# A gated mix of a state-space layer and an FFN on one core: slot 3 and the odd FFN tiles as pairs, another order at the start, the last read-out in two halves

## The chip, the core and the metric

The kernel runs on one core of a Trainium2 chip. Five engines work side by side, each through its own instructions in order, with semaphores between them: TensorE (PE; its weight loads are shown as PEld), VectorE (DVE), ScalarE (ACT), GpSimd (POOL) and SyncE (SP, which here only issues DMAs). Matmul results go to PSUM, which has eight banks of 128 x 512 float32 here; VectorE or ScalarE copies them out ("evicts" them) before a bank can be written again. The metric is the time of one execution on the device, in microseconds. The median of three runs of the kernel before is 145.91 us (145.41 to 146.05).

## What is computed

`x` has 2048 tokens of 448 features. Two branches are mixed by a gate per token: a diagonal complex state-space layer (a recurrence over the tokens with 448 states) and a feed-forward network with 1792 hidden features.

```python
x = A_x
g = _sigmoid((x * gate_w).sum(-1, keepdims=True))
# branch a
dt = exp(log_dt); Lam = Lambda_re + 1j * Lambda_im
Lam_bar = exp(dt * Lam)
B_bar = ((Lam_bar - 1.0) / Lam)[:, None] * (B_re + 1j * B_im)
Bu = einsum("bld,pd->blp", x, B_bar)
for t in range(L):
    h = Lam_bar[None, :] * h + Bu[:, t, :]
a = 2.0 * einsum("blp,dp->bld", hseq, Cmat).real + x * Dskip
# branch b
b = silu(x @ w1) @ w2
return g * a + (1 - g) * b
```

## The kernel before

**Tiling.** Tokens come in four chunks of 512 (`CH`), sixteen blocks of 128. The 448 states, real and imaginary, are seven slots of 128 partitions: slots 0, 1, 2 real and 4, 5, 6 imaginary parts of 384 states, slot 3 the last 64 states' real parts in its lower and imaginary parts in its upper 64 partitions. Slot 7 of `U` and `Gb` is slot 3 with its halves swapped. The FFN has fourteen tiles of 128 hidden features.

**The state-space branch.** For each chunk PE makes the seven slots of `B x` (BU), which are evicted to `U`. `lanes` (L659) then works on VectorE: products of `U` with cosines and sines of the states' phases turn the complex recurrence into a real one, seven `tensor_tensor_scan` instructions (L670) run it, ScalarE copies each scan result to `Gb` (L673), products turn it back into `H` (two buffers, by the chunk's parity). For each block of tokens, `readout` (L720) multiplies `H` with the read-out weights `CP` (L731), VectorE sums the result with the other branch (`tf`, L725; `ot`, L734), and SP stores it (L737). Each scan starts from the end of the chunk before.

**The FFN branch.** F1 makes the fourteen hidden tiles, ScalarE evicts them with Silu into `aT` (L695); F2 (`ffn2`, L700) multiplies them with `w2` for each block of tokens (fourteen matmuls, L706), ScalarE scales by 1 - g into `Tb` (L710).

**Pairs.** The contraction over 448 features is three and a half blocks of 128. `step` (L601) therefore makes two output tiles at a time with matmuls of 64 rows, two of which lie side by side in the array (L595). A pair's first half has eight matmuls, its second six: fourteen, against sixteen of half a block. The second half is emitted behind the first half of the next pair; `close` ends an open pair. A pair holds two PSUM banks from its first half until both tiles are evicted. Per chunk there are three BU pairs (0,1), (4,5), (6,2) and seven F1 pairs (k, 7 + k). Slot 3 is left over: `bu_last` (L639) makes it alone, with four matmuls over 128 rows (L644).

**The order of the work.** PE runs in the order in which the program adds its steps, written out by hand at the end (L796 to L862). The other engines' orders come from a planner (`Plan.order`, L102): with estimated costs it starts on each engine what can begin first, and of several that can begin at once the one with the lowest number `prio`. `Waits` then adds the semaphore waits. What an engine does is thus fixed in order, and an instruction that waits holds back all behind it.

**The start.** SP issues in order: the first 512 rows of x (one DMA, L372), B in four DMAs (L373 to L376), w1 in ten, w2 in one, then two transposing DMAs for chunk 1 of `xT` (L386), then C. ScalarE's queue issues the four parameter rows `prm` (L358). PE first runs 15 matmuls on zeros (`idle`, L415). Then it transposes x (L435; evicted at L439 to L443), then the parameters (L459, L461), for which VectorE first repeats 64 columns of `prm` (L453); then B: slots 0 and 1 (B01), two idle matmuls, slots 4 to 6 (B456). Then come BU(0,0), slots 2 and 3 (B23), the other BU pairs, F1(0,0), slot 3 and the gates of chunk 0. B's transposes are evicted at L576 (ScalarE) and L578 (VectorE) into `BT`. From the parameters, VectorE and ScalarE make phases `ph` and decays `rc` (L471 to L475); then ScalarE loads the table that has Silu and Sin (L476).

**The phases.** For each of four groups of states a ramp of 512 times the phase is made in `Gf`: b = 0 and 1 by ScalarE (L493), b = 2 and 3 by GpSimd (L496). VectorE takes the nearest whole number (L479) and subtracts it (L482); ScalarE takes the sine (L504, L507, L509), VectorE the absolute value (L511), ScalarE from that the cosine (L512). VectorE copies them for slots 4 to 6 (L514, L515).

**Lines at the seams.** `late_loads` (L392) issues the remaining x once chunk 0's swapped `Gb` is there. `swapped` (L634) copies slot 3 to slot 7 with two DMAs. `readout_weights` (L740) makes `CP` from C behind chunk 1's F1. The last seven lines of PE's order are F2(12), C(8), and so on to C(11), then C(12) to C(15) in a row: the last of these, its sum on VectorE and its store end the run.

Of the kernel before, what the change touches and what calls it, by code (L numbers as in the profile page):

```python
# [261 lines left out]
def bass_gated_mix__ssm_conv_s5__dense_activation_silu__prompt_kernel(nc, A_x, A_Lambda_re, A_Lambda_im, A_B_re, A_B_im, A_C_re, A_C_im,  # L262
               A_log_dt, A_Dskip, B_x, B_w1, B_w2, gate_w, out):
    with ExitStack() as ctx:
# [3 lines left out]
        def sb(name, shape, dtype):  # L268
            return E(nc.sbuf_tensor(name, list(shape), dtype))
# [34 lines left out]
        prm = sb("prm", [4, 512], BF16)  # L304
# [122 lines left out]
        def x_transposes(n):  # L427
            tk = Ps()

            def mm(pe):  # L430
                for q in range(2):
                    i = 2 * n + q
                    for b in range(4):
                        o = (q * 4 + b) * 128
                        r = pe.transpose(bk16(tk)[:, o:o + 128], xnat[:, b, XCOL[i]:XCOL[i] + 128], ident[:, :])  # L435
                return r
            P.add("pe", mm, ["xn0", "ident"], [tk], 0.5)
            if n == 0:
                DVE(lambda e: e.tensor_copy(xT[:, 0:2, 0:CH], bk16(tk)[:, :].rearrange("p (q n) -> p q n", q=2)),  # L439
                    [tk], ["xT00"], 0.7, 2)  # L440
            else:
                ACT(lambda e: e.activation(xT[:, 2, 0:CH], bk16(tk)[:, 0:CH], AF.Copy), [tk], ["xT01"], act_cost(512), 1)
                DVE(lambda e: e.tensor_copy(xT[:, 3, 0:CH], bk16(tk)[:, CH:2 * CH]), [tk, "xT01"], ["xT02"], 0.42, 2)  # L443

        x_transposes(0)
        x_transposes(1)

        def xr(tc):
            return [f"xT{tc}{k}" for k in range(2 if tc else 3)]


        prmn = [f"prm{k}" for k in range(4)]
        DVE(lambda e: e.tensor_copy(prm[:, 448:512], prm[:, 384:448]), prmn, ["prmd"], 0.2, 1)  # L453
        tk = Ps()

        def prm_t(pe, tk=tk):
            for b in range(4):
                lanes = prm[0:4, b:384:3] if b < 3 else prm[0:4, 384:512]
                pe.transpose(bk16(tk)[:, 4 * b:4 * b + 4], lanes, ident[0:4, 0:4])  # L459
            for b in range(3):  # L460
                r = pe.transpose(bk16(tk)[:, 16 + 4 * b:16 + 4 * b + 4], prm[0:4, 128 * b:128 * b + 128], ident[0:4, 0:4])  # L461
            return r
        P.add("pe", prm_t, prmn + ["prmd", "ident"], [tk], 0.3)
# [25 lines left out]
        for b in range(4):  # L489
            q = b % 2  # L490
            dst = Gf[:, b, :]
            if b < 2:
                ACT(lambda e, b=b, dst=dst: e.activation(dst, itf[:, :], AF.Copy, scale=ph[:, b:b + 1]),  # L493
                    ["itf", "ph"], [f"Gf{b}"], act_cost(512, 1), 2)
            else:
                POOL(lambda e, b=b, dst=dst: e.tensor_single_scalar(dst, itf[:, :], ph[:, b:b + 1], ALU.mult),  # L496
                     ["itf", "ph"], [f"Gf{b}"], 1.65)
            DVE(nearest(wk[q], dst), [f"Gf{b}"], [f"Gf{4 + q}"], dve_cost(512, 2), 3)
            DVE(minus(dst, dst, wk[q]), [f"Gf{b}", f"Gf{4 + q}"], [f"Gf{b}"], dve_cost(512), 3)
# [59 lines left out]
        def b_transposes(slots, reads, h, to_act):  # L559

            tk = Ps()
            n = len(slots)

            def mm(pe):
                for q in range(2):
                    i = 2 * h + q
                    for j, s in enumerate(slots):
                        o = (q * n + j) * 128
                        r = pe.transpose(bk16(tk)[:, o:o + 128], Bnat[:, s, XCOL[i]:XCOL[i] + 128], ident[:, :])  # L569
                return r  # L570
            P.add("pe", mm, reads + ["ident"], [tk], 0.06 * 2 * n)
            dst = BT[:, 2 * h:2 * h + 2, slots[0] * 128:(slots[-1] + 1) * 128]
            src = lambda: bk16(tk)[:, 0:2 * n * 128].rearrange("p (q m) -> p q m", q=2)
            name = f"BT{h}_{slots[0]}"
            if to_act:
                ACT(lambda e: e.activation(dst, src(), AF.Copy), [tk], [name], act_cost(256 * n), 0)  # L576
            else:
                DVE(lambda e: e.tensor_copy(dst, src()), [tk], [name], 0.1 + 0.00058 * 256 * n, 0)  # L578

        B01, B23, B456 = (0, 1), (2, 3), (4, 5, 6)  # L580
        b_transposes(B01, ["Bn0"], 0, False)
        b_transposes(B01, ["Bn0"], 1, True)
        idle(2)
        b_transposes(B456, ["Bn3"], 0, False)
        b_transposes(B456, ["Bn3"], 1, True)
        b01, b23, b456 = ([f"BT{h}_{s}" for h in range(2)] for s in (0, 2, 4))
# [4 lines left out]

        def half_steps(pe, w, xc, a, b, lo, hi, start):
            for i in range(len(lo)):
                for p0, (tk, c0), k in ((0, a, lo[i]), (64, b, hi[i])):
# [6 lines left out]
        def step(pair):  # L601

            w, tc, ca, cb, reads, evict = pair
            a, b = Ps("pair"), Ps("pair")
            xc = tc * CH
            begin = lambda pe: half_steps(pe, w, xc, (a, ca), (b, cb), (0, 1, 2, 3), (0, 1, 2, 3), True)
            end = lambda pe: half_steps(pe, w, xc, (b, cb), (a, ca), (0, 1, 2), (0, 1, 3), False)
            reads = reads + xr(tc)
            P.add("pe", begin, reads, [a, b], 0.87, rows=64)
# [28 lines left out]

        def bu_last(tc):  # L639
            tk = Ps()  # L640

            def mm(pe):
                for i in range(4):
                    r = pe.matmul(bk(tk), BT[:, i, 384:512], xT[:, i, tc * CH:(tc + 1) * CH],  # L644
                                  start=(i == 0), stop=(i == 3))
                return r
            P.add("pe", mm, b23 + ["BT3z"] + xr(tc), [tk], 0.87)
            u_out(3, tk)
            if tc:
                swapped(U, "U", 0)  # L650
            else:
                for k, p in ((0, 0), (1, 64)):
                    DVE(lambda e, p=p: e.tensor_copy(U[p:p + 64, 7, :], U[64 - p:128 - p, 3, :]),  # L653
                        ["U3"], [f"U7{'ab'[k]}"], dve_cost(512, 4), 2)
# [37 lines left out]
        def ffn1_pair(tc, k):  # L692
            def evict(a, b):
                for tk, fb in ((a, k), (b, 7 + k)):
                    ACT(lambda e, tk=tk, fb=fb: e.activation(aT[tc % 2][:, fb, :], bk(tk), AF.Silu),  # L695
                        [tk, "tbl"], [f"aT{tc % 2}_{fb}"], act_cost(512), 3)
            part = 0 if k < 3 else 1
            return w1s, tc, 128 * k, 896 + 128 * k, [f"w1{part}{n}" for n in range(5)], evict

        def ffn2(tb):  # L700
# [8 lines left out]
            P.add("pe", mm, ["w2"] + [f"aT{tc % 2}_{fb}" for fb in range(NFB)], [tk], 2.66)  # L709
# [10 lines left out]
        def readout(tb):  # L720
            tc, o = tb // 4, (tb % 4) * 128
            t0 = tb * 128
            tk = Ps("C")
# [5 lines left out]
            def mm(pe):  # L729
                for s in range(NSLOT):  # L730
                    r = pe.matmul(bk(tk)[:, 0:D_MOD], Ht[:, s, o:o + 128], CP[:, s, :], start=(s == 0), stop=(s == NSLOT - 1))  # L731
                return r
            P.add("pe", mm, [f"H{tc % 2}"] + [f"CP{s}" for s in range(NSLOT)], [tk], 1.33)
            DVE(lambda e, tk=tk: e.scalar_tensor_tensor(ot[tb % 3][:, :], bk(tk)[:, 0:D_MOD], g[:, tb:tb + 1],  # L734
                                                        tf[tb % 2][:, :], ALU.mult, ALU.add),
                [tk, f"g_{tc}", f"tf{tb % 2}"], [f"ot{tb % 3}"], dve_cost(448, 1, .05), 3)
            P.add("sp", lambda e: e.dma_start(out2[t0:t0 + 128, :], ot[tb % 3][:, :]), [f"ot{tb % 3}"], [], 0.55, 1,  # L737
                  outs[tb % 3], 128 * 896)

        def readout_weights(k):  # L740
            tk = Ps()

            def mm(pe, tk=tk, k=k):
# [5 lines left out]
            P.add("pe", mm, ["Cn0", "Cn1", "Cn2", "Cn3", "ident"], [tk], 0.5)  # L749
# [3 lines left out]
                [tk, "sc2"], ["ct0"], act_cost(448, 1), 8)  # L753
            if k < 3:
                ACT(lambda e, re=re, k=k: e.activation(ct[1][:, :], re(), AF.Copy, scale=sc2[:, k:k + 1]),
                    [tk, "sc2"], ["ct1"], act_cost(448, 1), 8)
            DVE(lambda e, re=re, k=k: e.scalar_tensor_tensor(CP[:, k, :], re(), sc1[:, k:k + 1], ct[0][:, :], ALU.mult, ALU.add),
                [tk, "sc1", "ct0"] + (["ct1"] if k < 3 else []), [f"CP{k}"], dve_cost(448, 1, .05), 15)
            if k < 3:
                DVE(lambda e, im=im, k=k: e.scalar_tensor_tensor(CP[:, 4 + k, :], im(), sc1[:, 4 + k:5 + k], ct[1][:, :], ALU.mult, ALU.add),  # L760
                    [tk, "sc1", "ct1"], [f"CP{4 + k}"], dve_cost(448, 1, .05), 15)

        def gates(tc):
# [9 lines left out]
            P.add("pe", mm, ["gwc", "gwc3"] + xr(tc), [tk], 0.6)  # L773
# [6 lines left out]
        def F1(tc, *ks):  # L780
            for k in ks:
                step(ffn1_pair(tc, k))

        def BU(tc, *ks):
            for k in ks:
                step(bu_pair(tc, k))
# [9 lines left out]
        BU(0, 0)  # L796
# [101 lines left out]
```

## Time and profile before

| What | us |
|---|---|
| median of three runs | 145.91 |
| profiled execution, its own time | 145.11 |
| its span, first to last instruction | 143.3 |
| TensorE busy | 138.5 |
| VectorE busy | 123.9 |
| ScalarE busy | 82.6 |
| first 512 rows of x landed (issued 0.73) | 4.03 |
| last parameter row landed | 4.97 |
| B_re and B_im of slots 0 to 2 and 4 to 6 landed | 4.86 and 6.55 |
| chunk 1's transposed x landed (two DMAs) | 21.44 and 21.96 |
| last store issued and landed | 141.27 and 142.93 |

A profile is one execution, taken by the hardware. Rows of a timeline name the start in us from the span's start, the duration, the engine, the line of the kernel, the operation, the tile written and those read, the shape, how many are merged into the row, and in brackets how long the engine was idle before and what ended that. Matmuls are pipelined and their ends are modelled, so that rows that follow each other overlap; the time that one takes of PE is the distance between starts. Landings are times at which a DMA's semaphore had its last update.

The granted TensorE clock is 1.00 throughout.

### The profile page before, as it was taken

The page shows a single profiled execution, that of the slowest core. Times are in us where ns is not written, and L with a number is a line of the kernel's source. Part 1 is how long each engine was busy: PE and PEld are TensorE (multiplying, and loading weights), DVE is VectorE, ACT ScalarE, POOL GpSimd, SP SyncE. Part 2 cuts the span into 40 slices and gives each one's busy share as a digit, 9 for nine tenths or more (in the row PEclk, how much of TensorE's full clock was granted, in tenths as well). Part 3 has the DMA queues.
Part 4 walks back from the last instruction along what each step waited for, and adds up shares of the span by engine and source line. Part 5 has one row for each costly group of instructions (what it writes and reads, how often), then busy time and mean ns, then how long its engine had stood idle before and what let it go on. Part 6 is the DMA issues. An engine that isn't in the chain of part 4 may idle for free.

```text
span 143.3 us, 2726 instructions
## 1 busy us (share of the span) xinstructions
PE 138.5 (97%) x1076; PEld 69.3 (48%) x1076; DVE 123.9 (86%) x144; ACT 82.6 (58%) x154; POOL 25.3 (18%) x62
## 2 busy tenths in 40 slices
PE   6899999999999999999999999999999999999991
PEld 4744543444446654444555554444455555555550
DVE  0459979999999999999799999969479999889592
ACT  3298799799778466978921134978811344411100
POOL 7176960000601300023170000040000000000000
PEclk9999999999999999999999999999999999999999
DMA  4999979015987000000011002000020021000022
GB/s 145 311 252 263 327 140 236 2 37 121 180 204 250 5 0 19 17 0 5 0 39 64 20 17 69 0 0 5 0 69 32 0 73 32 32 18 16 32 92 71
DMA packets 18165, 11.44 MB, mean 80 GB/s; under 512 B 8036, under 2 KB 17896, under 8 KB 18152
## 3 DMA queue, kind: packets, MB, share of 16 engines
q1 hardware_dynamic: 18144, 11.27, 31.1%
q8 instruction: 8, 0.13, 0.4%
q14 instruction: 5, 0.04, 0.1%
q10 hardware_dynamic: 8, 0.00, 0.0%
HBM read 6.94 MB, written 1.84 MB: 61 GB/s over the span
## 4 chain that ended last, share of the span: by engine, by line
PE 91%; ACT 5%; DVE 2%; issue 0%; DVEq 0%
PE ps L595 37%; PE ps L706 30%; PE ps L731 15%; PE ps L644 3%; PE ps L420 2%; ACT aT L695 2%; ACT COS L512 1%; PE ps L569 1%; PE ps L747 1%; PE ps L770 1%; PE ps L435 1%; DVE Gf L482 0%; DVE ot L734 0%; ACT SIN L507 0%; DVE U L653 0%
## 5 line engine op out<-in xcount | busy, mean ns | idle before, releaser
L706 PE MATMUL ps<-w2s,aT 128*128 128x448 bf16 x224 | 44.7, 353 | 0.0
L595 PE MATMUL ps<-xT,w1s 64*128 64x512 bf16 x392 | 43.8, 376 | 0.3 <-ACT aT L695 0.3
L695 ACT ACTIVATE aT<-ps 128x512 bf16<-128x512 f32 x56 | 29.6, 598 | 5.1 <-PE ps L595 5.1
L706 PEld LDWEIGHTS ps<-w2s,aT 128*128 128x128 bf16 x224 | 21.7, 98 | 20.4 <-issue 0.4
L595 PEld LDWEIGHTS ps<-xT,w1s 64*128 64x128 bf16 x392 | 18.9, 94 | 23.5 <-ACT aT L695 1.6
L710 ACT ACTIVATE Tb<-ps,g 128x448 bf16<-128x448 f32 x16 | 10.1, 633 | 32.6 <-PE ps L706 26.6
L670 DVE TENSOR_TENSOR_SCAN Gf<-rc,gin,PA 128x512 f32<-128x512 f32 x21 | 25.8, 1269 | 0.0
L731 PE MATMUL ps<-CP,H 128*128 128x448 bf16 x112 | 23.1, 353 | 0.0
L595 PE MATMUL ps<-xT,BT 64*128 64x512 bf16 x168 | 19.7, 377 | 0.0
L673 ACT ACTIVATE Gb<-Gf 128x512 bf16<-128x512 f32 x28 | 17.2, 628 | 3.8 <-DVE Gf L670 3.8
L624 ACT ACTIVATE U<-ps 128x512 bf16<-128x512 f32 x25 | 14.2, 596 | 3.2 <-PE ps L595 2.8
L734 DVE SCALAR_TENSOR_TENSOR ot<-ps,g,tf 128x448 bf16<-128x448 f32 x16 | 10.8, 677 | 6.0 <-PE ps L731 5.9
L731 PEld LDWEIGHTS ps<-CP,H 128*128 128x128 bf16 x112 | 10.9, 98 | 10.1
L595 PEld LDWEIGHTS ps<-xT,BT 64*128 64x128 bf16 x168 | 7.9, 94 | 10.1 <-ACT Tb L710 0.4
L679 POOL TENSOR_TENSOR k<-Gf,CC 128x7 f32<-128x7 f32 x3 | 2.8, 927 | 50.5 <-DVE Gf L670 50.5
L725 DVE SCALAR_TENSOR_TENSOR tf<-xnat,g,Tb 128x448 f32<-128x448 bf16 x16 | 10.7, 676 | 0.3
L657 DVE TENSOR_TENSOR PB<-Gb,SIN 128x1536 bf16<-128x1536 bf16 (+1 forms) x8 | 8.7, 1086 | 2.5 <-ACT Gb L673 2.3
L657 DVE TENSOR_TENSOR PB<-U,SIN 128x2048 bf16<-128x2048 bf16 (+1 forms) x8 | 8.4, 1083 | 0.1
L657 DVE TENSOR_TENSOR PA<-U,COS 128x3584 bf16<-128x3584 bf16 x4 | 8.1, 2018 | 0.1
L657 DVE TENSOR_TENSOR H<-PA,PB 128x3584 bf16<-128x3584 bf16 x4 | 8.1, 2026 | 0.1
L657 DVE TENSOR_TENSOR PA<-PA,PB 128x3584 bf16<-128x3584 bf16 x4 | 8.1, 2018 | 0.0
L657 DVE TENSOR_TENSOR PA<-Gb,COS 128x3584 bf16<-128x3584 bf16 x4 | 8.1, 2018 | 0.0
(98 smaller groups left out, 100.8 us busy)
## 6 DMA issues: line engine op xcount, KB each, us to landing
xnat<-in_A_x_dram SPq DMA_DIRECT2D x4, 448.0 KB, 4.8
out_dram<-ot SPq DMA_DIRECT2D x16, 112.0 KB, 1.7
w2s<-in_B_w_dram SPq DMA_DIRECT2D x1, 1568.0 KB, 9.9
w1s<-in_B_w_dram SPq DMA_DIRECT2D x3, 256.0 KB, 5.1
w1s<-in_B_w_dram SPq DMA_DIRECT2D x3, 192.0 KB, 4.4
Gb<-Gb SPq DMA_DIRECT2D x8, 64.0 KB, 1.9
Tb<-in_A_C_re_dram SPq DMA_DIRECT2D x1, 392.0 KB, 4.4
U<-U SPq DMA_DIRECT2D x6, 64.0 KB, 2.0
```

The costliest lines, as they stand in the source:

```text
L595: r = pe.matmul(bk(tk), w[p0:p0 + 64, k, c0:c0 + 128], xT[p0:p0 + 64, k, xc:xc + CH], start=(start and i == 0), stop=(not start and i == 2))
L624: ACT(lambda e: e.activation(U[:, s, :], bk(tk), AF.Copy), [tk], [f"U{s}"], act_cost(512), 4)
L644: r = pe.matmul(bk(tk), BT[:, i, 384:512], xT[:, i, tc * CH:(tc + 1) * CH], start=(i == 0), stop=(i == 3))
L657: return DVE(lambda e: e.tensor_tensor(o, a, b, op), r, w, dve_cost(n, 2), prio)
L670: DVE(lambda e, s=s, b=b, init=init: e.tensor_tensor_scan(Gf[:, s, :], rc[:, b:b + 1].to_broadcast([128, CH]), PA[:, s, :], init, ALU.mult ...
L673: ACT(lambda e, s=s: e.activation(Gb[:, s, :], Gf[:, s, :], AF.Copy), [f"Gf{s}"], [f"Gb{s}"], act_cost(512), 4)
L695: ACT(lambda e, tk=tk, fb=fb: e.activation(aT[tc % 2][:, fb, :], bk(tk), AF.Silu), [tk, "tbl"], [f"aT{tc % 2}_{fb}"], act_cost(512), 3)
L706: r = pe.matmul(bk(tk)[:, 0:D_MOD], aT[tc % 2][:, fb, o:o + 128], w2s[:, fb, :], start=(fb == 0), stop=(fb == NFB - 1))
L710: ACT(lambda e, tk=tk: e.activation(Tb[:, tb, :], bk(tk)[:, 0:D_MOD], AF.Copy, scale=g1[:, tb:tb + 1]), [tk, f"g1_{tc}"], [f"Tb{tb}"] + [f ...
L725: DVE(lambda e: e.scalar_tensor_tensor(tf[tb % 2][:, :], xnat[:, tb, :], g[:, tb:tb + 1], Tb[:, tb, :], ALU.mult, ALU.add), [f"xn{tc}", f" ...
L731: r = pe.matmul(bk(tk)[:, 0:D_MOD], Ht[:, s, o:o + 128], CP[:, s, :], start=(s == 0), stop=(s == NSLOT - 1))
L734: DVE(lambda e, tk=tk: e.scalar_tensor_tensor(ot[tb % 3][:, :], bk(tk)[:, 0:D_MOD], g[:, tb:tb + 1], tf[tb % 2][:, :], ALU.mult, ALU.add), ...
```

## The change

It has these parts.

1. The parameter rows lose the repeated 64 columns and the copy that made them (L453). The last group is transposed twice into the two halves of PSUM's partitions instead: eight small transposes for seven.
2. The transposes of x come in four groups of four (by halves of the 512 rows), each evicted whole: two by VectorE, two by ScalarE. Before there were two groups of eight, and the second was evicted by ScalarE and then VectorE.
3. In PE's order B456 moves behind the first half of the pair (0,1), and the gates of chunk 0 behind B23 and ahead of the pair (4,5). The memset of a part of `BT` that only `bu_last` read goes.
4. The ramp times phase for b = 0 and 1 is no longer made by ScalarE: VectorE multiplies and rounds in one instruction, subtracts the rounding constant in a second and takes the difference in a third.
5. `bu_last` goes. A pair is now made of any two tiles of BU or F1, of one chunk or of two: slot 3 is paired with an FFN tile, and FFN tile 6 of an even chunk with tile 13 of the next. Per two chunks there are 21 pairs for 20 pairs and two single tiles.
6. In chunk 0 slot 6 is evicted by VectorE too.
7. The last read-out (block 15) is made in two halves of 224 columns, each with its own PSUM bank, sum and store.
8. Read-out weights get other priorities in the planner (8 to 2 and 15 to 5), and some costs are given anew.

```diff
-            P.add("pe", mm, ["xn0", "ident"], [tk], 0.5)
+            P.add("pe", mm, ["xn0", "ident"], [tk], 0.24)
+            dst = xT[:, 2 * n:2 * n + 2, 256 * h:256 * h + 256]
+            src = lambda: bk16(tk)[:, 0:512].rearrange("p (q n) -> p q n", q=2)
             if n == 0:
-                DVE(lambda e: e.tensor_copy(xT[:, 0:2, 0:CH], bk16(tk)[:, :].rearrange("p (q n) -> p q n", q=2)),
-                    [tk], ["xT00"], 0.7, 2)
+                DVE(lambda e: e.tensor_copy(dst, src()), [tk], [f"xT00{h}"], 0.42, 0)
             else:
-                ACT(lambda e: e.activation(xT[:, 2, 0:CH], bk16(tk)[:, 0:CH], AF.Copy), [tk], ["xT01"], act_cost(512), 1)
-                DVE(lambda e: e.tensor_copy(xT[:, 3, 0:CH], bk16(tk)[:, CH:2 * CH]), [tk, "xT01"], ["xT02"], 0.42, 2)
+                ACT(lambda e: e.activation(dst, src(), AF.Copy), [tk], [f"xT01{h}"], act_cost(512), 0)
+        for h in range(2):
+            for n in range(2):
+                x_transposes(h, n)
...
-        DVE(lambda e: e.tensor_copy(prm[:, 448:512], prm[:, 384:448]), prmn, ["prmd"], 0.2, 1)
...
-            for b in range(4):
-                lanes = prm[0:4, b:384:3] if b < 3 else prm[0:4, 384:512]
-                pe.transpose(bk16(tk)[:, 4 * b:4 * b + 4], lanes, ident[0:4, 0:4])
+            for b in range(3):
+                pe.transpose(bk16(tk)[:, 4 * b:4 * b + 4], prm[0:4, b:384:3], ident[0:4, 0:4])
+            for h in range(2):
+                pe.transpose(bk16(tk)[64 * h:64 * h + 64, 12:16], prm[0:4, 384:448], ident[0:4, 0:4])
...
+        b_transposes(B01, ["Bn0"], 0, False)
+        b_transposes(B01, ["Bn0"], 1, True)
+        idle(2)
...
             if b < 2:
-                ACT(lambda e, b=b, dst=dst: e.activation(dst, itf[:, :], AF.Copy, scale=ph[:, b:b + 1]),
-                    ["itf", "ph"], [f"Gf{b}"], act_cost(512, 1), 2)
+                DVE(lambda e, b=b, t=t: e.tensor_scalar(t, itf[:, :], ph[:, b:b + 1], ROUND, ALU.mult, ALU.add),
+                    ["itf", "ph"], [f"Gf{4 + q}"], dve_cost(512, 2), 3)
+                DVE(lambda e, t=t: e.tensor_single_scalar(t, t, -ROUND, ALU.add), [], [f"Gf{4 + q}"], dve_cost(512, 2), 3)
+                DVE(lambda e, b=b, t=t, dst=dst: e.scalar_tensor_tensor(dst, itf[:, :], ph[:, b:b + 1], t, ALU.mult, ALU.subtract),
+                    ["itf", "ph", f"Gf{4 + q}"], [f"Gf{b}"], dve_cost(512), 3)
...
-        def step(pair):
-            w, tc, ca, cb, reads, evict = pair
+        def step(ta, tb):
+            (wa, xa, ca, ra, ea), (wb, xb, cb, rb, eb) = ta, tb
             a, b = Ps("pair"), Ps("pair")
+            begin = lambda pe: half_steps(pe, (wa, xa, a, ca), (wb, xb, b, cb), (0, 1, 2, 3), (0, 1, 2, 3), True)
+            end = lambda pe: half_steps(pe, (wb, xb, b, cb), (wa, xa, a, ca), (0, 1, 2), (0, 1, 3), False)
...
+        def bu(tc, s):
+            def evict(tk):
+                u_out(s, tk, tc == 0 and s in (1, 2, 5, 6))
+                if s == 3 and tc:
+                    swapped(U, "U", 0)
...
+        def f1(tc, fb):
+            def evict(tk):
+                ACT(lambda e: e.activation(aT[tc % 2][:, fb, :], bk(tk), AF.Silu),
+                    [tk, "tbl"], [f"aT{tc % 2}_{fb}"], act_cost(512), 3)
...
+            for c in ((slice(0, D_MOD),) if tb + 1 < NTB else (slice(0, 224), slice(224, D_MOD))):
+                n = c.stop - c.start
+                tk = Ps("C")
+                def mm(pe, tk=tk, c=c, n=n):
+                    for s in range(NSLOT):
+                        r = pe.matmul(bk(tk)[:, 0:n], Ht[:, s, o:o + 128], CP[:, s, c], start=(s == 0), stop=(s == NSLOT - 1))
+                    return r
...
+                P.add("sp", lambda e, c=c: e.dma_start(out2[t0:t0 + 128, c], ot[tb % 3][:, c]), [name], [], 0.55, 1,
+                      outs[tb % 3], 256 * n)
...
-        BU(0, 0)
+        BU(0, (0, 1))
+        b_transposes(B456, ["Bn3"], 0, False)
+        b_transposes(B456, ["Bn3"], 1, True)
         b_transposes(B23, ["Bn0", "Bn1", "Bn2"], 0, False)
         b_transposes(B23, ["Bn0", "Bn1", "Bn2"], 1, True)
-        DVE(lambda e: e.memset(BT[0:64, 3, 384:512], 0.0), ["BT1_2"], ["BT3z"], 0.2, 2)
-        BU(0, 1, 2)
-        F1(0, 0)
-        bu_last(0)
         gates(0)
-        F1(0, 1, 2, 3, 4, 5, 6)
+        BU(0, (4, 5), (6, 2))
+        step(bu(0, 3), f1(0, 7))
+        F1(0, (0, 8), (1, 9), (2, 10), (3, 11), (4, 12), (5, 13))
         lanes(0)
         late_loads()
         skip(0)
-        F1(1, 0, 1, 2)
+        step(f1(0, 6), f1(1, 13))
+        F1(1, (1, 7), (2, 8))
         close()
         F2(0)
-        bu_last(1)
-        BU(1, 0, 1, 2)
-        F1(1, 3, 4, 5, 6)
+        step(f1(1, 0), bu(1, 3))
+        BU(1, (0, 1), (4, 5), (6, 2))
+        F1(1, (3, 9), (4, 10), (5, 11), (6, 12))
         close()
...
-        BU(2, 0, 1, 2)
-        F1(2, 0, 1, 2, 3, 4, 5, 6)
+        BU(2, (0, 1), (4, 5), (6, 2))
+        step(bu(2, 3), f1(2, 7))
+        F1(2, (0, 8), (1, 9), (2, 10), (3, 11), (4, 12), (5, 13))
         close()
-        bu_last(2)
...
-        BU(3, 0, 1, 2)
-        F1(3, 0, 1, 2, 3, 4, 5, 6)
+        step(f1(2, 6), f1(3, 13))
+        step(f1(3, 0), bu(3, 3))
+        BU(3, (0, 1), (4, 5), (6, 2))
+        F1(3, (1, 7), (2, 8), (3, 9), (4, 10), (5, 11), (6, 12))
         close()
-        bu_last(3)
```

## The prediction, made before the changed kernel had run

> **What bounds the kernel now.** I read the page first, then the windows by stage, then TensorE's timeline, then ScalarE's and VectorE's for the start, and last the end of the run. Parts 1 and 4 of the page:
>
> ```profile
> PE 138.5 (97%) x1076; PEld 69.3 (48%) x1076; DVE 123.9 (86%) x144; ACT 82.6 (58%) x154; POOL 25.3 (18%) x62
> PE 91%; ACT 5%; DVE 2%; issue 0%; DVEq 0%
> ```
>
> TensorE is busy for 97% of the span and holds 91% of the chain that ended last. The windows (length; then busy time of PE, PEld, DVE, ACT, POOL; granted clock; DMA share; GB/s) say where the other 3% lie:
>
> ```profile
> 4.30:9.07 4.77, 4.26 (x64) 3.21 (x62) 3.11 (x14) 2.69 (x6) 1.48 (x7) 1.00 0.94 267
> 9.07:15.09 6.02, 6.02 (x64) 2.96 (x63) 4.91 (x12) 5.05 (x11) 4.59 (x10) 1.00 0.99 279
> 15.09:23.14 8.05, 7.73 (x75) 3.27 (x72) 6.88 (x11) 7.63 (x14) 5.08 (x16) 1.00 1.12 224
> 23.14:54.27 31.13, 31.13 (x270) 15.32 (x270) 30.64 (x29) 23.92 (x46) 4.13 (x6) 1.00 0.48 106
> ```
>
> From 23.14 us on PE has no idle time up to 140.5, and before that it lacks 0.51 and 0.32 us. So the time is PE's instruction stream, plus these two waits, plus a start and a tail: an edit pays where it takes matmuls out, closes a wait or shortens the tail. PE's timeline of the start (start, duration, line, shape, count, idle time before it and what ended it):
>
> ```profile
> 4.30 1.06 PE L435 MATMUL ps<-ident,xnat 128*128 128x128 bf16 x16
> 5.86 0.24 PE L459 MATMUL ps<-ident,prm 4*128 4x4 bf16 x4 [0.51 <-DVE prm L453]
> ...
> 6.78 0.83 PE L569 MATMUL ps<-ident,Tb 128*128 128x128 bf16 x12
> 7.55 1.04 PE L595 MATMUL ps<-xT,BT 64*128 64x512 bf16 x8
> 8.52 0.62 PE L569 MATMUL ps<-ident,Tb 128*128 128x128 bf16 x8
> 9.07 3.23 PE L595 MATMUL ps<-xT,BT 64*128 64x512 bf16 x28
> ...
> 12.98 0.83 PE L595 MATMUL ps<-xT,BT 64*128 64x512 bf16 x6
> 13.74 1.04 PE L644 MATMUL ps<-xT,BT 128*128 128x512 bf16 x4
> 14.62 0.54 PE L770 MATMUL ps<-gwc,xT 128*128 128x1 bf16 x16
> 15.09 7.73 PE L595 MATMUL ps<-xT,w1s 64*128 64x512 bf16 x70
> 23.14 6.87 PE L595 MATMUL ps<-xT,w1s 64*128 64x512 bf16 x62 [0.32 <-ACT aT L695]
> 29.93 2.82 PE L706 MATMUL ps<-w2s,aT 128*128 128x448 bf16 x14
> ```
>
> Ends overlap, so I count from start to start. In the second chunk 36 matmuls of 64 rows run from 54.27 to 58.16: 0.108 us each, 1.51 a pair of tiles, 0.86 its first half of eight, 0.65 its second of six. A transpose takes 0.056 (12 in 6.78 to 7.55, less the change of rows). A change between 64 and 128 rows costs about 0.1: the six matmuls from 12.98 hold PE 0.76 rather than 0.65. ScalarE at the start:
>
> ```profile
> 6.76 0.60 ACT L576 ACTIVATE BT<-ps 128x512 bf16<-128x512 bf16 x1 [0.77 <-PE ps L569]
> 7.65 0.81 ACT L576 ACTIVATE BT<-ps 128x768 bf16<-128x768 bf16 x1 [0.20 <-PE ps L569]
> 8.57 1.28 ACT L476 ACT_TABLE_LOAD   x1
> 10.36 1.32 ACT L493 ACTIVATE Gf<-itf,ph 128x512 f32<-128x512 f32 x2
> ```
>
> **Front, up to the pair (4,5).** Before, it begins at 9.07. Now: x transposes from 4.30, 16 x 0.056, to 5.2. The parameters (the last lands at 4.97) follow at once, since the copy at L453 that ended the 0.51 wait is gone; eight small transposes, some 0.28, to 5.48; B01 to 5.93, idle(2) to 6.15. There a new wait stands. The pair (0,1) needs slot 0's two copies. ScalarE gets two x copies of 0.60 in place of one (4.95 to about 6.1), then `dtc` (0.20; `pc` is ready near 5.8 and precedes the B copy), then BT1_0 (0.60, transposed by 6.1), done near 6.85. So PE stands 0.7 us and starts the pair at about 6.9 instead of 7.55. Everything behind it in PE's queue waits too: first half 0.86, change 0.1, 20 transposes 1.12 (B_im landed at 6.55, the last of B_re and B_im by 6.97), gates 0.47 as at 14.62 to 15.09, which hold the change back. That is 9.45. The B copy of 768 for (4,5) on ScalarE starts when its transposes end, near 8.7, and takes 0.81: ready near 9.6, after a table load that now runs from about 7.0 to 8.3. I take 9.6; if the load slips behind that copy there is no loss, if it slips ahead of it up to 1.28. Bounds 9.3 to 10.9. **Term: +0.55.**
>
> **From there to F2(0).** Before: 9.07 to 29.93, 20.86. Out go the single slot 3 with the gates and their changes (13.63, where the six would end, to 15.09: 1.46). The same 13 pairs remain: in the new order slot 3 and tile 7 are one pair, tile 6 goes with chunk 1's tile 13. The wait before 23.14 is 0.32 by modelled ends and 0.48 from start to start (0.69 between two couples, against 0.22); PE's banks were full because ScalarE did sines between evictions. ScalarE loses L493 (1.32) and U6 (0.60), gains x (0.60, before 6.2). I count the wait as gone; if it stays, 0.48 comes back. So 18.92, F2(0) at 28.5. **Term: -1.94; so far -1.39.**
>
> **Rest.** After F2(0), chunk 1 does a whole pair (1.51) for the single tile (32.59 to 33.55, 0.87 without the change of rows): +0.64. Chunks 2 and 3 trade two singles (69.48 to 70.35 and 102.35 to 103.23) for one pair: 1.51 - 1.75 = -0.24. **PE's end: -0.99.**
>
> **Tail.**
>
> ```profile
> 140.56 0.68 DVE L734 SCALAR_TENSOR_TENSOR ot<-ps,g,tf 128x448 bf16<-128x448 f32 x1 [0.69 <-PE ps L731]
> ```
>
> The 14 matmuls of 224 columns take what seven of 448 took (0.095 for 0.189, above the 0.056 at which transposes with their loads follow each other). After PE's last matmul VectorE has 224 elements: L511, the same operation, takes 1.22 for 1024, so an element costs (1.22 - 0.68)/576 = 0.94 ns, and 0.68 less 224 of them is 0.47: **-0.21**; the first half's sum (0.47) lies under the second's matmuls, behind tile 14's sum that ends 0.3 before it must start. SP issues one DMA more (0.34), done before the last. Landing: 112 KB takes 1.7 us in the DMA view; half has no row. Below: 448 KB of x takes 4.8, so 0.009 us per KB and 0.5 less; above: the 64 KB copies of U take 2.0, so 0.3 more. I take 1.7 as it is, that row being the nearest.
> The Trainium skill (DMA: Bandwidth & Descriptors, Specifications) holds against the halves that runs under 512 B are read, modified and written; these have 448 B. If that doubled the bytes moved, my estimate from that page would be 112 KB again and the landing unchanged; no row of this trace isolates it.
>
> **Costed at nothing.** Phase products on VectorE: `tensor_scalar` with a column operand has no row; nearest are L479's 0.42 to 0.53, above it L482's 0.69 and below it 0.38 (two of L479 in 0.75). With one more L479 and a 0.69 in place of L482, VectorE gains 2 x 0.42 and U6's 0.69, some 1.5 us, and gets `ph` at 6.95 rather than 8.34, with no wait for ScalarE until 10.4. It is covered by VectorE's idle time (0.89 before 10.54, 0.84 before 20.19) and by slack: the last H is ready at 132.4, read-out 12 starts near 135.0. Without cover it would delay H by 1.5 and still fit. Slot 3 of chunk 3 moreover comes near 90 and not at 103.4, so the 2.58 us that VectorE waited at 104.75 go. The read-out weights' new priorities reorder ScalarE and VectorE alone, and PE runs through that stage without idle time. Loads keep their order and SP's queue; the x transposes of chunk 1 land at 21.44 and 21.96, and pair (6, 13 of chunk 1) now wants them at 23.2, 24.66 before: 1.2 us of margin, which also caps what the front could gain beyond my sum. "x in one load" changes no load in the diff: the first 512 rows were one DMA already.
>
> **Sum.** 0.55 - 1.94 + 0.64 - 0.24 - 0.21 = -1.20 on a span of 143.3, profiled time 145.11: 143.9. The runs' median, 145.91, stands 0.8 above the profiled execution; I carry that over: **144.7**. A measurement of this kernel tells about 0.5% (0.73 us) from no change.
>
> **Rivals.** (1) *Given back at the front*: the wait for B copies replaces the parameter wait at a higher price. Against it: copies and table load fit my times; for it: every step from 5.2 to 9.6 hangs on ScalarE's order. With (4,5) at 10.2 and the 23.14 wait kept, -1.20 + 0.6 + 0.48 = -0.1: 145.8, no change. (2) *Slower, ScalarE in F1*: the sine block (1.06 + 0.63 + 1.15 + 0.72 + 1.15 = 4.7 us) goes ahead of Silu evictions. Spread between 15.4 and 22.6 it cost 0.48. In one piece it holds evictions 4.7 us; eight banks less the four of the open and the beginning pair leave two pairs, 3.0 us, so PE stalls 1.7, and 2.9 where a U eviction and a Gb copy (0.6 each) join it. It decides from 2.0 us of stall; at 2.5: 145.91 - 1.20 + 2.5 = 147.2. Against it: phases start 1.4 us earlier and Gf0 and Gf1 come about 11, well before Gf2 and Gf3. (3) *Halves don't pay*: tail -0.21 + 0.3, so 145.0; still faster. (4) *Front better than I see*: (4,5) at 9.3 and landing 0.5 shorter: 143.9.
>
> **Chances.** Forecast with (3) and (4) 0.66, rival (1) 0.20, rival (2) 0.14. Faster by over 0.5% 0.66, within 0.20, slower 0.14. The likeliest case alone spans 143.9 to 145.1; for eight in ten I reach from 143.5 (both of (4), 0.4 for the spread of runs) to 146.1, the upper edge of case (1).
>
> **What would show it.** PE runs from the x transposes into the parameters without the 0.51, and waits instead about 0.7 before slot (0,1) near 6.9; gates start near 9.0; (4,5) begins near 9.6; F2(0) near 28.5; no idle of PE after 10; 588 matmuls of 64 rows and none of L644; PE ends near 139.5; the last VectorE sum takes 0.47; VectorE's wait near 104 is gone. I am wrong if PE idles between 10 and 29 behind ScalarE, or if the pair (6, 13) waits for the transposed x.

## The result and the profile after

The changed kernel is slower by half a per cent: its median is 146.85 us (16 runs, 145.93 to 147.15), that of the kernel before 145.95 (16 runs, 145.25 to 146.28); ratio 1.0054, 95% interval 1.0037 to 1.0071. The forecast was 144.7, and faster. The profiled execution took 146.40 us over a span of 144.4 (before: 145.11 over 143.3).

The page after, parts 1 and 4:

```profile
PE 139.2 (96%) x1096; PEld 71.3 (49%) x1096; DVE 125.4 (87%) x146; ACT 82.0 (57%) x152; POOL 27.5 (19%) x62
PE 53%; DVE 8%; issue 3%; POOL 1%; ACT 1%
```

The second line has changed its nature. Before, 91% of the chain that ended last was PE; now the chain followed back from the end leaves PE at 65.8 us and goes through ScalarE, VectorE's scans and read-out weights and GpSimd's small instructions to 46.5 us. So at one place in the middle PE waited for all of these. The stages, from start to start of PE's rows in both profiles:

| Stage | before | after | difference | forecast |
|---|---|---|---|---|
| up to the pair (4,5) | 9.07 | 10.35 | +1.28 | +0.55 |
| (4,5) to F2(0) | 20.86 | 18.88 | -1.98 | -1.94 |
| F2(0) to chunk 2's first pair | 24.34 | 24.98 | +0.64 | +0.64 |
| chunk 2's first pair to read-out 0 | 16.89 | 17.66 | **+0.77** | -0.87 |
| read-out 0 to chunk 3's first pair | 15.98 | 15.99 | +0.01 | 0 |
| chunk 3's first pair to read-out 4 | 16.09 | 16.72 | +0.63 | +0.64 |
| read-out 4 to PE's end | 37.25 | 37.28 | +0.03 | 0 |
| PE's end to the end of the span | 2.85 | 2.51 | -0.34 | -0.21 |

Two rows are off: the start by 0.73 and chunk 2 by 1.64. The windows of chunk 2 (length; busy time of PE, PEld, DVE, ACT, POOL; clock; DMA), first of the kernel before:

```profile
54.27:71.16 16.89, 16.89 (x178) 7.96 (x178) 15.58 (x18) 14.68 (x29) 2.31 (x4) 1.00 0.04 9
```

and of the changed kernel:

```profile
54.21:71.87 17.66, 16.88 (x173) 7.25 (x173) 17.54 (x20) 15.75 (x31) 2.18 (x4) 1.00 0.06 16
```

PE now idles there by its modelled ends for 0.78; from start to start the excess is 1.64, in five places from 57.90 to 65.77. VectorE works nearly the whole stage.

**Where that comes from.** The changed kernel's GpSimd timeline, then its VectorE's, then its ScalarE's (start, duration, engine, line, what, idle time before and what ended it):

```profile
28.42 0.65 POOL L585 COPY SS<-s 128x3 f32<-128x3 f32 x1 [16.52 <-ACT s L556]
41.96 0.40 POOL L583 COPY CC<-c 128x4 f32<-128x4 f32 x1 [6.70 <-ACT c L558]
48.15 0.23 POOL L582 TENSOR_SCALAR sc<-cw 128x4 f32<-128x4 f32 x1
```

```profile
18.71 0.17 DVE L553 TENSOR_SCALAR ph<-ph 128x4 f32<-128x4 f32 x1
...
44.35 2.09 DVE L649 TENSOR_TENSOR PB<-U,SIN 128x2048 bf16<-128x2048 bf16 x2
49.67 0.68 DVE L752 SCALAR_TENSOR_TENSOR CP<-ps,sc,ct 128x448 bf16<-128x448 bf16 x1 [3.23 <-issue]
```

```profile
41.59 0.30 ACT L558 ACTIVATE c<-pha,hpi 128x8 f32<-128x8 f32 x1
...
43.64 1.57 ACT L686 ACTIVATE aT<-ps 128x512 bf16<-128x512 f32 x3 [0.43 <-PE ps L598]
48.41 0.63 ACT L747 ACTIVATE ct<-ps,sc 128x448 f32<-128x448 bf16 x1 [3.19 <-POOL sc L582]
...
64.11 0.63 ACT L665 ACTIVATE Gb<-Gf 128x512 bf16<-128x512 f32 x1 [0.23 <-DVE Gf L662]
64.65 2.04 ACT L686 ACTIVATE aT<-ps 128x512 bf16<-128x512 f32 x4
```

The same places in the kernel before, one row of VectorE, two of ScalarE and one of GpSimd:

```profile
8.38 0.20 DVE L521 TENSOR_SCALAR ph<-ph 128x4 f32<-128x4 f32 x1
13.16 0.30 ACT L526 ACTIVATE c<-pha,hpi 128x8 f32<-128x8 f32 x1
45.67 0.67 ACT L752 ACTIVATE ct<-ps,sc 128x448 f32<-128x448 bf16 x1
20.02 0.23 POOL L549 TENSOR_SCALAR sc<-cw 128x3 f32<-128x3 f32 x1
```

Read them as one chain. The phase over a whole chunk (`ph[4:8]`, L553; three VectorE instructions of 0.2 us) and from it its sine `s8`, its absolute value `pha` and from that its cosine `c8` on ScalarE (L556 to L558) have the planner's priority 12: nearly everything of the start goes ahead of them. Before, VectorE made that phase from 8.38 to 9.65, and `c8` came at 13.16. Now VectorE begins it at 18.71, ScalarE has `s8` at 28 and `c8` at 41.59, behind evictions. GpSimd's chain of small instructions from them to the scale factors of the read-out weights (`sc1`, `sc2`) ended at 20.25 before and at 48.38 now. The first read-out weight is due at 45. ScalarE and VectorE stand before it, 3.19 and 3.23 us, each with its whole queue behind: on VectorE chunk 1's sum and scans, on ScalarE the copies of their results. Those copies (L665) are then still to come when PE makes chunk 2's pairs, stand in ScalarE's queue ahead of evictions and wait for the scans. PE's banks fill, and PE stops, at last before this row of its timeline:

```profile
65.77 5.35 PE L598 MATMUL ps<-xT,w1s 64*128 64x512 bf16 x48 [0.67 <-ACT aT L686]
```

The start, in PE's timeline:

```profile
4.35 1.42 PE L436 MATMUL ps<-ident,xnat 128*128 128x128 bf16 x16
5.70 0.23 PE L482 MATMUL ps<-ident,prm 4*128 4x4 bf16 x3
...
7.54 1.04 PE L598 MATMUL ps<-xT,BT 64*128 64x512 bf16 x8 [0.56 <-DVE ph L510]
8.51 1.29 PE L463 MATMUL ps<-ident,Tb 128*128 128x128 bf16 x20
9.64 0.54 PE L765 MATMUL ps<-gwc,xT 128*128 128x1 bf16 x16
10.35 3.39 PE L598 MATMUL ps<-xT,BT 64*128 64x512 bf16 x29 [0.17 <-ACT BT L470]
```

The wait for the parameters is gone, the new wait ahead of (0,1) is there (0.83 from start to start, where 0.11 would do), and a second one of 0.31 ahead of (4,5). Each x transpose of the first seven took 0.107 us here and 0.056 in the profile before, 0.36 in sum; the last section says more of that.

### The profile page after: what moved, and what is told of

It is laid out like the page before. It is cut to its first block, busy times and chain, and to the rows that moved or that the text cites. A ratio compares the mean times of both kernels' runs of the same rounds, so it can differ in the third digit from the quotient of the medians.

```text
span 144.4 us, 2759 instructions
## 1 busy us (share of the span) xinstructions
PE 139.2 (96%) x1096; PEld 71.3 (49%) x1096; DVE 125.4 (87%) x146; ACT 82.0 (57%) x152; POOL 27.5 (19%) x62
## 4 chain that ended last, share of the span: by engine, by line
PE 53%; DVE 8%; issue 3%; POOL 1%; ACT 1%
PE ps L697 22%; PE ps L598 15%; PE ps L725 15%; DVE Gf L662 4%; DVE CP L755 1%; DVE PA L649 1%; DVE CP L752 1%; POOL cw L561 1%; ACT aT L686 1%; PE ps L765 1%; ACT Gb L665 0%; DVE ot L729 0%; POOL sc L582 0%; POOL sc L581 0%; POOL gin L510 0%
## 5 line engine op out<-in xcount | busy, mean ns | idle before, releaser
L598 PE MATMUL ps<-xT,w1s 64*128 64x512 bf16 x392 | 47.8, 376 | 0.7 <-ACT aT L686 0.7
L598 PEld LDWEIGHTS ps<-xT,w1s 64*128 64x128 bf16 x392 | 20.8, 94 | 24.2 <-ACT aT L686 1.6
L598 PE MATMUL ps<-xT,BT 64*128 64x512 bf16 x196 | 26.0, 376 | 0.8 <-DVE ph L510 0.6
L725 PE MATMUL ps<-CP,H 128*128 128x448 bf16 (+1 forms) x119 | 23.2, 342 | 0.0
L665 ACT ACTIVATE Gb<-Gf 128x512 bf16<-128x512 f32 x28 | 17.2, 629 | 10.6 <-DVE Gf L662 10.5
L729 DVE SCALAR_TENSOR_TENSOR ot<-ps,g,tf 128x448 bf16<-128x448 f32 (+1 forms) x17 | 11.1, 653 | 6.7 <-PE ps L725 6.6
L598 PEld LDWEIGHTS ps<-xT,BT 64*128 64x128 bf16 x196 | 10.8, 94 | 12.2 <-issue 0.9
L725 PEld LDWEIGHTS ps<-CP,H 128*128 128x128 bf16 x119 | 11.5, 98 | 9.8 <-issue 0.4
L630 ACT ACTIVATE U<-ps 128x512 bf16<-128x512 f32 x24 | 13.4, 597 | 1.7 <-PE ps L598 1.7
```

What stands on the lines that cost most here:

```text
L598: r = pe.matmul(bk(tk), w[p0:p0 + 64, k, c0:c0 + 128], xT[p0:p0 + 64, k, xc:xc + CH], start=(start and i == 0), stop=(not start and i == 2))
L630: ACT(lambda e: e.activation(U[:, s, :], bk(tk), AF.Copy), [tk], [f"U{s}"], act_cost(512), 4)
L665: ACT(lambda e, s=s: e.activation(Gb[:, s, :], Gf[:, s, :], AF.Copy), [f"Gf{s}"], [f"Gb{s}"], act_cost(512), 4)
L725: r = pe.matmul(bk(tk)[:, 0:n], Ht[:, s, o:o + 128], CP[:, s, c], start=(s == 0), stop=(s == NSLOT - 1))
L729: DVE(lambda e, tk=tk, c=c, n=n: e.scalar_tensor_tensor(ot[tb % 3][:, c], bk(tk)[:, 0:n], g[:, tb:tb + 1], tf[tb % 2][:, c], ALU.mult, ALU ...
```

## The experiments

Theory A is the chain just told. Its rivals: B, the read-out weights' new priorities put them ahead of chunk 1's scans and cause the stall; C, the pairs overload ScalarE in chunk 2 whatever the start does. All ratios are to the kernel before, run on the same chip, with 95% intervals.

**The six instructions early.** The changed kernel, priority 12 to 1.

```diff
-        DVE(... ph[:, 4:8] ... ["ph"], ["ph5"], 0.2, 12)
+        DVE(... ph[:, 4:8] ... ["ph"], ["ph5"], 0.2, 1)
...
-        ACT(... c8[:, :], pha[:, :], AF.Sin ... ["c8"], 0.3, 12)
+        ACT(... c8[:, :], pha[:, :], AF.Sin ... ["c8"], 0.3, 1)
```

> The changed kernel with one edit: the six small instructions of the phase over 512 tokens (three on VectorE, s8, pha and c8 on ScalarE) get priority 1 in the planner in place of 12. Theory A (these six slid to 18.7 to 41.6 us because the new start leaves VectorE and ScalarE no hole for them; GpSimd's scale factors for the read-out weights then come at 48.4, ScalarE and VectorE wait 3.2 us for them in order, chunk 1's scans and copies slide, and PE stands 1.6 us behind ScalarE between 57 and 66): c8 near 12, scale factors before 25, no wait of ScalarE for L582, PE's stage from BU(2) to the first read-out 16.0 us in place of 17.7, time 1.6 us below the changed kernel, ratio to the kernel before 0.993 to 0.996. Rival B (the read-out weights' new priorities, which put them ahead of chunk 1's scans, cause the stall): stage still above 17.2, ratio 1.003 to 1.006.

0.9953 (0.9929 to 0.9976), median 144.84. Its GpSimd timeline has the last scale factors at 16 us, and its window of chunk 2 has no idle PE:

```profile
16.13 0.75 POOL L582 TENSOR_SCALAR sc<-cw 128x4 f32<-128x4 f32 x1
```

```profile
54.00:70.03 16.03, 16.03 (x174) 7.54 (x174) 15.90 (x17) 13.33 (x26) 2.18 (x4) 1.00 0.06 15
```

The stage is 16.03 as the forecast had it, the read-out weights' priorities being the new ones: A holds, B falls. Between the ratios 1.0054 and 0.9953 lie 1.5 us.

**The old priorities of the read-out weights.**

```diff
-                [tk, "sc2"], ["ct0"], act_cost(448, 1), 2)
+                [tk, "sc2"], ["ct0"], act_cost(448, 1), 8)
...
-                ... [f"CP{k}"], dve_cost(448, 1, .05), 5)
+                ... [f"CP{k}"], dve_cost(448, 1, .05), 15)
```

> The changed kernel with the read-out weights' old priorities (8 on ScalarE, 15 on VectorE). Theory A: the scale factors still come near 48, so a wait of some us stays on ScalarE or VectorE and PE stands again between 54 and 72; ratio 1.001 to 1.008. Rival B: the stall goes, stage from BU(2) to the first read-out 16.0 us, ratio 0.993 to 0.996.

1.0454 (1.0400 to 1.0508), far above what either theory expected; the four executions took 151.51, 151.85, 153.43 and 153.90 us. The scale factors came at 49.2, the last read-out weight fell behind the whole of chunk 1's recurrence (74.9 us), and PE waited for it at read-out 0. Its PE timeline:

```profile
71.39 0.95 PE L765 MATMUL ps<-gwc,xT 128*128 128x1 bf16 x32
75.59 1.64 PE L725 MATMUL ps<-CP,H 128*128 128x448 bf16 x7 [3.24 <-DVE CP L752]
77.02 4.40 PE L697 MATMUL ps<-w2s,aT 128*128 128x448 bf16 x14
```

So the new priorities, far from causing the stall, kept the late factors from costing five times as much: 1.0454 less the early version's 0.9953 is 7.3 us, where the changed kernel loses 1.5. The third row is a second price of the wait: see the last section.

**The phase products on ScalarE again**, in the changed kernel (its part 4 undone).

```diff
-                DVE(... e.tensor_scalar(t, itf[:, :], ph[:, b:b + 1], ROUND, ALU.mult, ALU.add) ...)
-                DVE(... e.tensor_single_scalar(t, t, -ROUND, ALU.add) ...)
-                DVE(... e.scalar_tensor_tensor(dst, itf[:, :], ph[:, b:b + 1], t, ALU.mult, ALU.subtract) ...)
+                ACT(... e.activation(dst, itf[:, :], AF.Copy, scale=ph[:, b:b + 1]) ... act_cost(512, 1), 2)
...
+            DVE(nearest(wk[q], dst) ... dve_cost(512, 2), 3)
+            DVE(minus(dst, dst, wk[q]) ... dve_cost(512), 3)
```

> The changed kernel with the products of phases 0 and 1 on ScalarE again. Theory A: VectorE has its hole back, s8 and c8 come before 16 us, scale factors before 25, and the stall in chunk 2 is gone without any priority touched: ratio 0.993 to 0.997, less what ScalarE's 1.3 us cost at the start (the pair (4,5) up to 0.6 later, a wait of up to 0.5 near 22). Rival B: the stall stays, ratio 1.003 or above. Rival C (the pairs of slot 3 in chunk 2 overload ScalarE there, whatever the start does): the stall stays too.

0.9953 (0.9928 to 0.9977), 144.98. `c8` came at 13.9, the scale factors at 18.9, the stage of chunk 2 took 16.03. This is the second way to the same end, with no priority touched: the products on VectorE had filled the hole in which the planner used to put the six instructions. C falls as well, since the pairs of chunk 2 are all there. And the ratio equals that of the six early with the products on VectorE, so part 4 of the change has no gain of its own that shows. PE's window from the pair (4,5) to F2(0) has no idle time here either, though ScalarE makes the products again:

```profile
10.87:29.76 18.89, 18.89 (x175) 9.79 (x175) 18.48 (x25) 16.03 (x32) 7.18 (x24) 1.00 0.77 180
```

**The lateness alone, in the kernel before.**

```diff
-            DVE(... ph[:, 4:8], ph[:, 0:4], 512.0, ALU.mult), ["ph"], ["ph5"], 0.2, 12)
+            DVE(... ph[:, 4:8], ph[:, 0:4], 512.0, ALU.mult), ["ph", "SINd"], ["ph5"], 0.2, 12)
```

> The kernel before with one more dependency: the phase over 512 tokens waits for the copied sines, so that s8 and c8 slide on ScalarE behind chunk 1's F1 as in the changed kernel. Nothing else is touched. Theory A: c8 near 40 us, scale factors near 46 to 48, ScalarE waits for L550 some 2 to 3 us, and PE gets a stall between 54 and 72 that it did not have: 1 to 4 us, ratio 1.007 to 1.03 (the old priorities of the read-out weights cost more in e2 than the new ones). If the lateness is harmless by itself and only the new order or the pairs make it hurt: 1.000.

1.0128 (1.0093 to 1.0162), 147.48. Its ScalarE timeline has the same two rows as the changed kernel's, and in its window of chunk 2 PE idles too (18.36 long with 17.32 busy; 16.89 long before, all busy):

```profile
42.15 0.30 ACT L526 ACTIVATE c<-pha,hpi 128x8 f32<-128x8 f32 x1
...
50.13 0.63 ACT L752 ACTIVATE ct<-ps,sc 128x448 f32<-128x448 bf16 x1 [3.79 <-POOL sc L550]
```

```profile
54.78:73.14 18.36, 17.32 (x177) 7.73 (x177) 18.27 (x21) 16.24 (x32) 2.31 (x4) 1.00 0.03 8
```

No pair, no read-out and nothing of PE's order was changed there; on ScalarE and VectorE, beside the six, one instruction each changed its place. The lateness is enough.

**The last read-out in halves, alone in the kernel before.**

```diff
-            tk = Ps("C")
+            for c in ((slice(0, D_MOD),) if tb + 1 < NTB else (slice(0, 224), slice(224, D_MOD))):
+                tk = Ps("C")
...
-            P.add("sp", lambda e: e.dma_start(out2[t0:t0 + 128, :], ot[tb % 3][:, :]) ...)
+                P.add("sp", lambda e, c=c: e.dma_start(out2[t0:t0 + 128, c], ot[tb % 3][:, c]) ...)
```

> The kernel before with the last read-out in halves alone. My sum of the prediction: 0.21 us less from VectorE's last sum and the landing as before, ratio 0.9985. In the profile of the changed kernel the time from PE's end to the end of the span was 2.51 us, 2.85 before: ratio 0.9977. If rows of 448 B cost more than they save: 1.000 or above.

0.9969 (0.9950 to 0.9989). The last sum took 0.45, its row in the changed kernel's timeline being

```profile
141.89 0.45 DVE L729 SCALAR_TENSOR_TENSOR ot<-ps,g,tf 128x224 bf16<-128x224 f32 x1 [0.17 <-PE ps L725]
```

The part gains 0.2 to 0.7 us. The two halves' stores landed 1.54 and 1.61 us after their issue in the changed kernel and both 1.54 here, the last whole row's 1.66 in the kernel before. These times spread: in four of the nine profiles with halves the last store took 1.74 to 1.78, and among those with whole rows the one of the lateness experiment took 1.82. The Trainium skill's line on runs under 512 B (DMA: Bandwidth & Descriptors, Specifications) has no cost that shows beside this spread.

**The pairs alone, in the kernel before.** Parts 5 and 6 with the old start.

```diff
-        F1(0, 0)
-        bu_last(0)
+        step(bu(0, 3), f1(0, 7))
...
-        F1(0, 1, 2, 3, 4, 5, 6)
+        F1(0, (0, 8), (1, 9), (2, 10), (3, 11), (4, 12), (5, 13))
...
-        F1(1, 0, 1, 2)
+        step(f1(0, 6), f1(1, 13))
+        F1(1, (1, 7), (2, 8))
...
-        bu_last(1)
+        step(f1(1, 0), bu(1, 3))
```

and likewise in chunks 2 and 3.

> The kernel before with the pairs alone: slot 3 and the odd FFN tiles paired as in the change, slot 6 of chunk 0 on VectorE, all else and the order of the start as before (gates behind slot 3's pair). My sum: four single slots of 0.87 us become two pairs of 1.51, and one change of rows less: 0.46 to 0.65 us less, ratio 0.9955 to 0.997; if the wait near 22 goes as well, 0.993. A rival that has the pairs themselves overload ScalarE in chunk 2 expects no gain or a loss, 1.000 or above, with PE's stage from BU(2) to the first read-out above 16.9 us.

1.0074 (1.0045 to 1.0102): a loss, against my sum and not by rival C's way, for chunk 2's stage took 16.03. PE lost its time at the start. Its PE timeline, and below it ScalarE's:

```profile
19.85 1.68 PE L595 MATMUL ps<-xT,w1s 64*128 64x512 bf16 x14 [0.23 <-ACT aT L683]
22.90 8.38 PE L595 MATMUL ps<-xT,w1s 64*128 64x512 bf16 x76 [1.36 <-ACT aT L683]
```

```profile
17.13 1.05 ACT L504 ACTIVATE SIN<-Gf 128x1024 bf16<-128x1024 f32 x1
18.08 0.62 ACT L507 ACTIVATE SIN<-Gf 128x512 bf16<-128x512 f32 x1
18.60 0.71 ACT L509 ACTIVATE SIN<-Gf,sturn 128x512 bf16<-128x512 f32 x1
19.21 0.58 ACT L683 ACTIVATE aT<-ps 128x512 bf16<-128x512 f32 x1
19.69 2.18 ACT L512 ACTIVATE COS<-Gf,hpi 128x1024 bf16<-128x1024 f32 x2
```

The sines and cosines run almost in one piece from 17.13 to 21.87, with one eviction between them: the mechanism of rival (2), in a kernel where nobody had looked for it. PE stood 1.74 and 0.61 us from start to start, less 0.22 each: 1.9 us. The changed kernel has no such wait; its sines run at 12.57, 14.08 and 17.82, its cosines at 15.81 and 20.12, with evictions between. That VectorE makes the first phases there is not the reason: with them on ScalarE again (the third experiment) the sines run at 12.92, 14.60 and 16.14, the cosines at 19.13 and 20.65, and PE has no wait either. Which other part of the new start does it was not tried.

**Pairs and halves, in the kernel before.** Both edits just shown.

> The kernel before with the pairs and the last read-out in halves, the start as before. If the two gains add up: e5's ratio less 0.003, near 0.993. Beside e1_early (0.9953; the whole change with the six instructions early) it prices the new start: equal if the start costs nothing, lower if the new start is a loss.

1.0047 (1.0024 to 1.0069), with the same wait of 1.74. Beside 0.9953 for the whole change with the six instructions early, the new start is worth some 1.4 us, though by its own rows up to (4,5) it loses time: it pays between there and F2(0), where the sines no longer stand in one block (18.89 us against 21.45, of which some 0.5 is the gates that the new start does earlier). The stages of the matmuls behind F2(0) are equal in both profiles to 0.02 us, so the read-out weights' priorities, in which the two also differ, have no part in it.

**B456 back ahead of (0,1).** The change with the six early, with two edits:

```diff
+        b_transposes(B456, ["Bn3"], 0, False)
+        b_transposes(B456, ["Bn3"], 1, True)
...
-        ACT(lambda e: e.preload_act_table_set("silu_and_others"), [], ["tbl", "dtc", "rc"], 1.3, 2)
+        ACT(lambda e: e.preload_act_table_set("silu_and_others"), ["BT1_4"], ["tbl", "dtc", "rc"], 1.3, 2)
...
         BU(0, (0, 1))
-        b_transposes(B456, ["Bn3"], 0, False)
-        b_transposes(B456, ["Bn3"], 1, True)
```

> e1_early with B456 back ahead of the pair (0,1) in PE's order, and the table load behind the copy for the pair (4,5) on ScalarE. In e1_early PE stands 0.83 - 0.11 us ahead of (0,1) and 0.33 ahead of (4,5), with 12 transposes (0.67) in between: they should fill the first wait. Theory: (4,5) starts 0.6 to 0.9 us earlier than e1_early's 10.13, ratio 0.989 to 0.992, below every other version. If ScalarE's copies are the limit whatever PE's order, no change from e1_early: 0.995.

0.9909 (0.9882 to 0.9937), 144.27. PE's timeline:

```profile
6.63 0.38 PE L420 MATMUL ps<-PB 128*128 128x256 bf16 x2
6.85 0.83 PE L463 MATMUL ps<-ident,Tb 128*128 128x128 bf16 x12
7.61 1.04 PE L600 MATMUL ps<-xT,BT 64*128 64x512 bf16 x8
8.58 0.62 PE L463 MATMUL ps<-ident,Tb 128*128 128x128 bf16 x8
9.04 0.54 PE L767 MATMUL ps<-gwc,xT 128*128 128x1 bf16 x16
9.52 3.41 PE L600 MATMUL ps<-xT,BT 64*128 64x512 bf16 x29
```

The twelve transposes stand in the wait for (0,1), and (4,5) starts at 9.52 in place of 10.35. From the x transposes to its end PE has no wait left. That version is faster than both kernels, and a second set of runs on another chip agrees:

> e7_b456back once more, as the neighbour of e9_noidle on the same chip: 0.988 to 0.994 again.

0.9897 (0.9869 to 0.9926), 144.35.

**Without the two idle matmuls.** The version before, with

```diff
         b_transposes(B01, ["Bn0"], 1, True)
-        idle(2)
         b_transposes(B456, ["Bn3"], 0, False)
```

> e7_b456back without the two idle matmuls on zeros behind B01. There PE has no wait left behind them (no gap between starts above 0.32 us after 4.3), so their 0.22 us lie on the path if ScalarE's copies for (0,1) and (4,5) are early enough: 0.1 to 0.2 us less, ratio 0.001 to 0.0015 below e7's; if the copies end the wait instead, PE waits 0.2 us ahead of (0,1) and the time stays.

0.9883 (0.9857 to 0.9908), 144.02, against 0.9897 of its neighbour: the intervals overlap almost wholly, and its profile shows a wait of 0.22 us ahead of (0,1), in an execution whose x transposes all ran at 0.107. Not decided.

## Why the prediction was wrong

**The step that failed** is in "Costed at nothing": that the phase products on VectorE are "covered by VectorE's idle time (0.89 before 10.54, 0.84 before 20.19)", and that "PE runs through that stage without idle time". I counted the first hole as empty. The same list of VectorE's rows has the chunk's phase at 8.38, 9.29 and 9.49, beside that hole: work of priority 12 that got in because nothing better was ready. Filling the hole with 1.5 us of better priority moved it out by ten microseconds, and `c8` on ScalarE by 28; I asked what waits for the products and never who had used the hole. What it put in place is 1.64 us of PE in chunk 2, which the early, the ScalarE and the late experiments show from both sides. The two signs by which I would have known myself wrong, idle time between 10 and 29 and a wait of pair (6, 13), look elsewhere: after the wait that ended at 10.35 both stayed away.

**The front** was mis-sized, +0.55 against +1.28. Of the 0.73, 0.36 are the x transposes at half the rate in this execution, which is no effect of the change (below). The rest: the eight small transposes took 0.44 where I had 0.28, ScalarE's B copy began 0.14 after `dtc` (6.80), and PE began the pair 0.14 after that copy's end (7.40), so that (0,1) came another 0.3 later; (4,5) then waited 0.31 for its copy. The mechanism, a wait for B copies where the transposes had been, was right, and its cure is the experiment with B456 back ahead of (0,1).

**Right**: the numbers between the two. From (4,5) to F2(0), -1.98 for -1.94, with the wait near 22 gone. That term is in part luck: I had the wait go because ScalarE loses L493 and an eviction, but the third experiment puts the products back on ScalarE and has no wait, and the pairs alone, with that eviction gone from ScalarE, have a longer one. Then +0.64 and +0.63 where a pair replaces a single tile; 16.03 for chunk 2 in every version that has the pairs and not the late factors, against 16.89 less 0.87. The tail gained more than I took, -0.34: 0.23 by VectorE's sum, some 0.05 ahead of it and 0.05 on the store. VectorE's wait near 104 shrank from 2.58 to 0.92 and did not go; nothing hung on it. The transposed x (landed 20.98) and pair (6, 13) never met.

**Rivals.** (1), given back at the front, came in part. (2) had the right mechanism, evictions held behind other work in ScalarE's order, and the wrong place: not the sines in chunk 0 but chunk 1's copies in chunk 2. With the pairs alone it came just as described. That the parts' prices do not add up, -1.20 by my sum and a loss for the pairs by themselves, was in no case of mine.

**The base.** I carried over that the median stands 0.8 above the profiled execution. That difference is now 0.45 for the changed kernel. The clock's start, early in the profile before, may be part of it; how much was not measured.

## What to carry to other kernels

When an engine's idle time is to cover new work, list what already runs in that hole, down to instructions of 0.2 us, and follow each to its last reader: in an order made by priorities the unimportant goes where there is room, and without room it goes last. A small instruction that gates a later stage needs a due time, not a low priority. And a part of a change is priced within the order that it makes: the same pairs cost 1.9 us of waiting for ScalarE with the old start and nothing there with the new one.

## What the runs showed of the hardware that was not expected

- **When TensorE's clock rises differs from execution to execution.** All begin PE's dummy matmuls at 1.18 us. The trace's clock records begin at 4.24 us in the profile before and at 5.09 in the one after, and between 4.07 and 7.09 in the other profiles; until then a 128-column transpose takes 0.107 us, from then on 0.056. The windows print 1.00 for both times, and so did I ("1.00 throughout"); here the distance between starts tells the clock and the printed share doesn't. The Trainium skill (TensorE: Matmul & The Clock Gate, Part 1: The HAM clock gate) says that the gate looks at a free-running window of 3413 ns, so that the change comes at a different point each time; these starts agree.
- **After a wait of 3.4 us the clock was halved for 3.4 us.** With the old priorities PE stood from 72.19 to 75.59 from start to start; from 77.02 on matmuls of 448 columns took 0.37 us in place of 0.189 (clock record 0.5 from 76.8 to 80.2). The same section puts the fall at one idle window. The length agrees: the clock records of all twelve profiles, but for each one's last, are 3.413 us long or whole multiples of it. The idleness does not quite: on that grid the window that ended at 76.8 began at 73.4, and PE ran seven matmuls in it from 75.59 on. Two of the four executions, this one among them, had a mean clock of 0.989, the two longer ones 0.977; a second such window is my estimate for these. The longest wait in the other versions was 1.74 us, and none of them shows a fall before PE's end.
- **VectorE's `tensor_scalar` on 512 float32 keeps no one time.** With two constants it took 0.41 to 0.44 us, and 0.53 in the old start's first row. With a column of phases (L522) it took 0.49 and 0.92 in the changed kernel and 0.47 to 0.56 in four other profiles; the subtraction of a constant behind it (L524) took 0.41 in some rows and 0.69 to 0.80 in others. What lengthens them was not tried.
- **GpSimd's small instructions spread.** A copy of 128 x 3 took 0.19 to 1.18 us before and 0.18 to 2.03 in the changed kernel, the longest at 42.45, while VectorE ran its products. The profile's spans on GpSimd are rough, and what slows it was not tried.
